# A recurrence and a feed-forward network on one core: the keys turned by one block transposition and a trip through DRAM

## The chip, the cores and the metric

The kernel runs on one core of a Trainium2 chip. The metric is device microseconds of one execution; lower is better. TensorE multiplies matrices, VectorE and ScalarE work element by element on 128 partitions, SyncE (SP) issues most transfers.

## The reference

For 4 batches of 8 heads, with 768 steps in time and 48 numbers a head, a state of 48 x 48 is decayed by rows and updated at each step, and read with the query. The outputs of all heads together are the rows of x, 3072 x 384, for a feed-forward network with 2048 hidden units.

```
for t in range(S):
    state = alpha[:, :, t, :, None] * state + einsum('bhd,bhe->bhde', k[:, :, t], v[:, :, t])
    y[:, :, t] = einsum('bhd,bhde->bhe', q[:, :, t], state)
x = y.transpose(0, 2, 1, 3).reshape(B * S, H * D)
h = x @ w_in
out = (0.5 * h * (1.0 + erf(h / sqrt(2)))) @ w_out
```

All inputs and the output are float32.

## The kernel before

**The attention.** The work is cut into 24 units: 12 groups of 256 steps (three for each batch), each in two units of four heads. A unit holds two tiles of 128 partitions, 64 for each head (48 in use). VectorE makes running products of alpha forward and backward (L314, L327), multiplies queries (L320) and keys (L333) with them, and the recurrence becomes products of matrices over chunks of 64 steps. In `scores` (L354) keys meet queries; VectorE masks the result (`masked`, L400). In `inside`, the masked scores meet the values (L423), and the keys meet the values (L441), which gives what each chunk adds to the state. For L441 the keys must lie with time on the partitions; this turned form is the tile kn. VectorE adds the states up (`chain`, L461), and in `outside_part` (L491) the states meet the queries. ScalarE copies the outputs out (`y_out`, L571), to free the bank of PSUM for the next scores; they become rows of x in two parts, a rounded one and a rest (L563, L567).

**How the keys are turned.** Units 0 to 5 use TensorE (L362) and a copy by ScalarE. Units 6 to 23 (FLIPPED = 6) use VectorE: `flipped` (L373) transposes 32 x 32 blocks, four of them in one instruction, from one group of 32 partitions to another. 16 instructions turn one unit; the plan places them in pairs ("flip").

**The feed-forward network.** Weights and activations are split into a rounded part and a rest, and three products are added. Rows 0 to 1023 go in blocks of 256 rows (L599, L691), the rest in wide blocks of 512 (L616, L634). A step is a first product, two passes of the activation on ScalarE (L668, L672), the rest of the activation on VectorE (L681, glo), and a second product. A wide block has 16 steps of 18 matmuls of 512 columns.

**The order of work.** All of it is written out ahead: a planner in the kernel gives each operation a cost (the table COST, in us), the operations that it waits for, and a rank, and simulates the engines. The order that comes out is the order in which the instructions are issued on TensorE, VectorE, ScalarE and SP. From unit 6 on TensorE visits the attention for the old state of unit n-2, `inside` of unit n-1 and the scores of unit n close together, and works on the network between these visits. When a unit's rows of x may be written depends on the network: the wide blocks have two buffers. Loads of later units and the transfers that spread rows of x over partitions (x<-z, L589) are issued by SP in the plan's order.

Of the kernel before, what the change touches and what calls it, by code (L numbers as in the profile page):

```python
# [8 lines left out]
F32 = mybir.dt.float32  # L9
# [16 lines left out]
FLIPPED = 6  # L26
# [9 lines left out]
SLOW = 1.0  # L36
COST = dict(
    turn=0.3, head=0.75, body=0.95, tail=0.49, sel=0.6, sel2=1.0, ends=0.22, differ=1.2, half=0.34, minus=0.4, gminus=0.35, rest=0.5, rest2=1.0,
    scan=0.65, scan2=0.65, back0=0.86, back=0.71, times=0.62, q=1.35, scores=1.24, scores1=0.69, flip=0.54, kn=0.52, mask=0.62, mask1=0.4, kn1=0.36, inside=1.28, chain=1.1, outer=0.77, carry=0.22,
    xh=0.6, xl=0.72, spread=2.0, check=0.85, load=2.6, fetch=0.4, u=1.0, c0=0.56, c1=0.89, c2=0.56, c3=0.95, c4=0.92,  # L40
    hi=0.82, lo=0.89, gemm1=2.12, gelu=0.51, low=0.62, most=1.4, last=0.69, part=1.0,
    wide1=2.1, wide2=2.07, wpart=1.1,
# [5 lines left out]
def gla_then_gelu_ffn(ctx: ExitStack, tc: tile.TileContext, q, k, v, alpha, qg, kg, ag, vg, w_in, w_out, out):  # L48
    nc = tc.nc
    B, H, D, S = q.shape  # L50
    NF, P, NK, _ = w_in.shape
# [5 lines left out]
    NCH = G // CS  # L57
    DP = 64
    NPAIR = H // 2
    NU = NPAIR // 2  # L60
    DR = DP - D
    QUAD = P // 4
# [9 lines left out]
    const = ctx.enter_context(tc.tile_pool(name="const", bufs=1))  # L72
    work = ctx.enter_context(tc.tile_pool(name="work", bufs=3))
    ffn = ctx.enter_context(tc.tile_pool(name="ffn", bufs=2))
    ps_s = ctx.enter_context(tc.tile_pool(name="ps_s", bufs=1, space=PSUM))
    y_cm = tc.tile_pool(name="ps_y", bufs=1, space=PSUM, side="right")
    ps_y = y_cm.__enter__()
# [43 lines left out]
    def y_of(n):  # L121
        return (ybank, sbank)[n % 2] if n < SPLIT else sbank
# [10 lines left out]
    cur = {}  # L133
# [31 lines left out]
    mask = const.tile([P, CS], F32, name="mask")  # L165
    nc.gpsimd.memset(mask, 1.0)
    for half in range(2):
        r = slice(half * CS, (half + 1) * CS)
        nc.gpsimd.affine_select(  # L169
            out=mask[r],  # L170
            in_=mask[r],
# [47 lines left out]
    for f2 in range(NF2):  # L219
        src = w_in[2 * f2 : 2 * f2 + 2].rearrange("two p c f -> p two (c f)")  # L220
        pieces.append((src, wi_hi[f2], wi_lo[f2]))
        src = w_out[2 * f2 * P : (2 * f2 + 2) * P, :].rearrange("(two p) e -> p two e", p=P)
# [114 lines left out]
    def ends_batch(g, j):  # L337
        return g % GPB == GPB - 1 and j == NCH - 1

    def scores(g, u):  # L340
        d = cur[g, u]
        n = NU * g + u
        d["s"] = s_of(n)
        if n >= SPLIT:
            d["s"] = [
                ps_h().tile([P, BANK], F32, tag="hp", name=f"sh_{n}"),
                ps_w().tile([P, BANK], F32, tag="sw", name=f"sw_{n}"),
            ]
        for j in range(NCH):
            for i in range(2):  # L350
                t, o = slice(j * CS, (j + 1) * CS), slice(i * CS, (i + 1) * CS)
                for h in range(2):
                    r = slice(h * DP, h * DP + D)
                    nc.tensor.matmul(  # L354
                        d["s"][h][o, t], lhsT=d["kt"][r, (2 * j + i) * CS : (2 * j + i + 1) * CS], rhs=d["qt"][r, i, t], start=True, stop=True
                    )

    def turned(g, u):
        d = cur[g, u]
        for j in range(NCH):  # L360
            e = (2 + j % 2) * C
            nc.tensor.transpose(  # L362
                out=d["s"][j // 2][:, e : e + C], in_=d["kt"][:, 2 * j * CS : 2 * (j + 1) * CS], identity=ident
            )

    def flipped(g, u, src, dsts):

        k5 = cur[g, u]["kt"].rearrange("p (j i a t) -> p i a j t", j=NCH, i=2, a=2)
        n5 = kn_tile(g, u).rearrange("p h (j b d) -> p h b j d", j=NCH, b=2)
        r = slice(src * QUAD, (src + 1) * QUAD)  # L370
        for dst in dsts:
            o = slice(dst * QUAD, (dst + 1) * QUAD)
            nc.vector.transpose(out=n5[o, src // 2, src % 2], in_=k5[r, dst // 2, dst % 2])  # L373

    def room(n):
        return stage if n % 2 and n < NU * NSB else work

    def kn_tile(g, u):
        d = cur[g, u]
        if "kn" not in d:  # L380
            pool = room(NU * g + u)
            d["kn"] = pool.tile([P, 2, 2 * P], F32, tag="kn", bufs=2 if pool is work else 1, name=f"kn_{g}_{u}")
        return d["kn"]
# [23 lines left out]
    def inside(g, u):  # L407
        d = cur[g, u]
        ybank = y_of(NU * g + u)
        vn = vbuf[g % NB]  # L410
        spare = () if g else (0, 1)[: u + 1]
        for i in spare:
            nc.tensor.matmul(
                ybank[:, i, :G], lhsT=zeros, rhs=products[:, :G], start=True, stop=False, skip_group_check=True
            )
        for j in range(NCH):
            for i in range(2):
                r = slice(i * CS, (i + 1) * CS)
                for h in range(2):
                    rows = D if i in spare else DP  # L420
                    o = slice((h ^ i) * DP, (h ^ i) * DP + rows)
                    e = (2 * u + h) * D
                    nc.tensor.matmul(  # L423
                        ybank[o, i, j * CS : (j + 1) * CS],
                        lhsT=vn[r, j, e : e + rows],
                        rhs=d["ss"][r, h, j, :],
                        start=(j == 0 and i not in spare),
                        stop=(j == 0 and g % GPB == 0),
                        skip_group_check=True,
                    )  # L430
        kn = d["kn"].rearrange("p b (c h d) -> p b c h d", c=2, h=2)
        for j in range(NCH):
            if ends_batch(g, j):
                continue
            t = 2 * C + j * D
            for i in range(2):
                r = slice(i * CS, (i + 1) * CS)
                for h in range(2):
                    o = slice(h * DP, (h + 1) * DP)
                    e = (2 * u + h) * D  # L440
                    nc.tensor.matmul(  # L441
                        ybank[o, i, t : t + D],
                        lhsT=d["kn"][r, h, j * DP : (j + 1) * DP] if NU * g + u >= FLIPPED else kn[r, j // 2, j % 2, h],
                        rhs=vn[r, j, e : e + D],
                        start=False,
                        stop=True,
                        skip_group_check=True,
                    )
# [400 lines left out]
    def op(*args, **kw):  # L849
        ops.append(Op(*args, **kw))  # L850
        return ops[-1]
# [4 lines left out]
    def plan_unit(n):  # L856
        g, u = divmod(n, NU)
        d = unit[n] = {}
        p, pp_ = unit.get(n - 1, {}), unit.get(n - 2, {})
        r = unit_rank[n]  # L860
# [23 lines left out]
        shared = [pp_.get("out", pp_["xh"]), pp_.get("out", pp_["xl"])] if NU <= n <= SPLIT else []  # L884
        of_y = [yp.get("out", yp.get(x)) for x in ("xh", "xl")]
        if n >= FLIPPED:
            for src in range(4):
                for dsts in ((0, 1), (2, 3)):
                    d["kn"] = op("DVE", "flip", lambda src=src, dsts=dsts: flipped(g, u, src, dsts), [d["keys"], pp_["inside"]], rank=r)
            d["scores"] = op("PE", "scores1", lambda: scores(g, u), [d["keys"], d["q"], sp.get("mask"), sp.get("kn") if n < FLIPPED + NU else None, *shared], rank=r)  # L890
        else:
            d["scores"] = op("PE", "scores", lambda: (scores(g, u), turned(g, u)), [d["keys"], d["q"], sp.get("mask"), sp.get("kn"), *shared], rank=r)
# [27 lines left out]
        else:  # L920
            d["mask"] = op("DVE", "mask", lambda: masked(g, u), [d["scores"], rp.get("inside")], rank=-1)
            d["kn"] = op("ACT", "kn", lambda: turned_out(g, u), [d["scores"], rp.get("inside"), d["mask"]], rank=-1)
        d["inside"] = op("PE", "inside", lambda: inside(g, u), [d["mask"], *of_y], rank=r)
        if n >= NU:
            d["inside"].deps.append(d["kn"])
# [77 lines left out]
    for n in range(n_units):  # L1003
        plan_unit(n)
# [224 lines left out]
    t = 0.0  # L1229
    idle = 0  # L1230
    while True:
        moved = False
        for e in ("DVE", "ACT", "PE", "SP", "POOL"):
            if free_at[e] <= t + 1e-9:
                o = choose(e, t)
# [13 lines left out]
        t = min(later_on)  # L1249
# [8 lines left out]
    for o in plan:  # L1258
# [5 lines left out]
        out=outside[:, n_units:],  # L1264
# [90 lines left out]
```

## Time and profile before

| | |
|---|---|
| three runs | 497.4, 499.94, 499.95 us; median 499.94 us |
| the profiled execution | 500.8 us, of which the span of the profile is 499.1 us |
| granted clock of TensorE over the span | 0.995 |
| TensorE, matmuls | busy 482.2 us, 5144 instructions |
| VectorE | busy 336.3 us, 773 instructions |
| ScalarE | busy 192.2 us, 381 instructions |
| transfers | 44.31 MB, mean 89 GB/s |

Busy times are unions of the time in which an engine has an instruction under way. Matmuls are pipelined and their ends are modelled, so a new one starts long before the one before it ends. In the rows, PE is TensorE, PEld its weight loads, DVE VectorE, ACT ScalarE; L373 is line 373 of the kernel.

### The profile page before, as it was taken

To read this page: it belongs to the slowest core of one execution; us is meant where nothing else is said; L and a number is where in the kernel's file an instruction comes from. 1 tells how busy PE (TensorE), PEld (TensorE's weight loads), DVE (VectorE), ACT (ScalarE), POOL (GpSimd) and SP (SyncE) were. 2 spreads that over 40 slices of the span, in tenths; PEclk is the share of its full clock that TensorE was granted. 3 is DMA by queue.
4 is the path that set the end of the run, shared out by engine and by line. 5 is a ranking of instruction groups with operands and counts; after the bars stand their busy time and mean duration, and the time that the engine had idled before them with its cause. 6 is when DMAs were issued, how large, how long until landed. Compare 5 with 4: busy or idle time off the path is not lost.

```text
span 499.1 us, 12166 instructions
## 1 busy us (share of the span) xinstructions
PE 482.2 (97%) x5144; PEld 409.2 (82%) x5144; DVE 336.3 (67%) x773; ACT 192.2 (39%) x381; POOL 7.4 (1%) x21
## 2 busy tenths in 40 slices
PE   7999999999999999999999999999999999999993
PEld 5678999999989999777788777778778888888882
DVE  6898998989999999999943999941751111211112
ACT  4788765243343334332423343232432222322221
POOL 2000000000000000000000000000000000000000
PEclk9999999999999999999999999999999999999997
DMA  8996662322232232313200622000100000100001
GB/s 299 393 348 198 247 211 71 108 78 85 85 93 97 92 110 71 130 54 107 73 1 1 198 69 88 4 1 1 70 24 5 1 1 0 65 0 0 1 0 69
DMA packets 20845, 44.31 MB, mean 89 GB/s; under 512 B 2832, under 2 KB 4688, under 8 KB 20784
## 3 DMA queue, kind: packets, MB, share of 16 engines
q1 hardware_dynamic: 19136, 38.41, 22.9%
q0 software_dynamic: 880, 3.93, 2.0%
q10 hardware_dynamic: 768, 1.11, 0.7%
q8 instruction: 42, 0.69, 0.5%
q14 instruction: 19, 0.16, 0.1%
HBM read 36.57 MB, written 4.72 MB: 83 GB/s over the span
## 4 chain that ended last, share of the span: by engine, by line
PE 51%; DVE 29%; DMA 7%; issue 6%; ACT 4%; ACTq 1%; SPq 0%; DVEq 0%
PE hw L616 22%; PE accw L634 22%; DVE kn L373 10%; DMA st<-in_moe_w_out_dram 5%; DVE glo L681 4%; DVE pp L314 3%; DVE rp L327 2%; PE hp L599 2%; DVE state L461 2%; PE acc L691 1%; DVE kd L333 1%; DMA x<-z 1%; DVE ss L400 1%; DMA ad<-in_ag_dram 1%; DVE x L567 1%
## 5 line engine op out<-in xcount | busy, mean ns | idle before, releaser
L681 DVE TENSOR_TENSOR glo<-hw,ghi 128x512 fp32r<-128x512 f32 x64 | 44.1, 689 | 133.2 <-ACT hw L672 132.8
L616 PE MATMUL hw<-x,wih 128*128 128x512 f32 x384 | 121.2, 396 | 0.6 <-DVE ss L400 0.6
L668 ACT ACTIVATE ghi<-hw 128x512 fp32r<-128x512 f32 x64 | 38.3, 599 | 176.6 <-PE hw L616 176.6
L373 DVE STREAM_TRANSPOSE kn<-kd 32x128 f32<-32x128 f32 x288 | 87.1, 303 | 4.4
L616 PEld LDWEIGHTS hw<-x,wih 128*128 128x128 f32 x384 | 71.4, 188 | 17.9 <-PE hw L616 1.0
L634 PE MATMUL accw<-ghi,woh 128*128 128x512 f32 x192 | 76.3, 398 | 0.0
L616 PE MATMUL hw<-x,wil 128*128 128x512 f32 x192 | 75.8, 395 | 0.0
L634 PE MATMUL accw<-ghi,wol 128*128 128x512 f32 x192 | 75.2, 392 | 0.0
L599 PE MATMUL hp<-x,wih 128*128 128x256 f32 x384 | 69.7, 282 | 0.0
L599 PEld LDWEIGHTS hp<-x,wih 128*128 128x128 f32 x384 | 59.9, 188 | 0.5 <-issue 0.2
L634 PE MATMUL accw<-glo,woh 128*128 128x512 f32 x192 | 56.7, 397 | 0.8 <-DVE glo L681 0.8
L599 PE MATMUL hp<-x,wil 128*128 128x256 f32 x192 | 53.6, 280 | 0.0
L691 PE MATMUL acc<-woh,ghi 128*128 128x384 f32 x128 | 44.0, 344 | 0.8 <-ACT ghi L668 0.8
L616 PEld LDWEIGHTS hw<-x,wil 128*128 128x128 f32 x192 | 36.0, 187 | 8.8
L691 PE MATMUL acc<-wol,ghi 128*128 128x384 f32 x128 | 43.1, 337 | 0.0
L634 PEld LDWEIGHTS accw<-ghi,woh 128*128 128x128 f32 x192 | 36.0, 187 | 8.5
L634 PEld LDWEIGHTS accw<-glo,woh 128*128 128x128 f32 x192 | 35.4, 188 | 8.8 <-DVE glo L681 1.2
L634 PEld LDWEIGHTS accw<-ghi,wol 128*128 128x128 f32 x192 | 36.1, 188 | 7.7
L668 ACT ACTIVATE ghi<-hp 128x512 fp32r<-128x512 f32 x32 | 19.1, 596 | 55.4 <-PE hp L599 46.0
L672 ACT ACTIVATE hw<-hw 128x512 f32<-128x512 f32 x64 | 37.9, 593 | 0.0
L599 PEld LDWEIGHTS hp<-x,wil 128*128 128x128 f32 x192 | 36.1, 188 | 0.0
L314 DVE TENSOR_TENSOR_SCAN pp<-ad,bottom 128x256 f32<-128x256 f32 x48 | 31.5, 680 | 4.6 <-POOL mask L169 3.5
(136 smaller groups left out, 584.6 us busy)
## 6 DMA issues: line engine op xcount, KB each, us to landing
st<-in_moe_w_in_dram SPq DMA_DIRECT2D x8, 768.0 KB, 7.4
st<-in_moe_w_out_dram SPq DMA_DIRECT2D x8, 768.0 KB, 7.7
qd<-in_qg_dram SPq DMA_DIRECT2D x23, 256.0 KB, 3.1
ad<-in_ag_dram SPq DMA_DIRECT2D x23, 256.0 KB, 3.0
kd<-in_kg_dram SPq DMA_DIRECT2D x23, 256.0 KB, 3.5
vn<-in_vg_dram SPq DMA_DIRECT2D x12, 416.0 KB, 4.7
out_dram<-parts POOLq DMA_DIRECT2D x3, 768.0 KB, 3.8
x<-z SPq DMA_DIRECT2D x60, 32.0 KB, 2.0
```

The source lines that it names most:

```text
L314: nc.vector.tensor_tensor_scan(pp[:, i], at[:, i], bottom, MID, ALU.mult, ALU.max)
L327: nc.vector.tensor_tensor_scan(rp[:, i, G - 2 :: -1], at[:, i, G - 1 : 0 : -1], bottom[:, 1:], rp[:, i, G - 1 :], ALU.mult, ALU.max)
L333: nc.vector.tensor_tensor(out=k4, in0=k4, in1=cur[g, u]["rp"].rearrange("p i (j t) -> p i j t", j=NCH), op=ALU.mult)
L373: nc.vector.transpose(out=n5[o, src // 2, src % 2], in_=k5[r, dst // 2, dst % 2])
L461: d["chain"] = nc.vector.tensor_tensor(out=st[j + 1], in0=new, in1=st[j], op=ALU.add)
L599: nc.tensor.matmul(hp[:, j, :], lhsT=a[:, j, i * P : (i + 1) * P], rhs=x[:, i, :], start=(start and m == 0), stop=(stop and (j, i, n) in t ...
L616: nc.tensor.matmul(h, lhsT=a[:, j, i * P : (i + 1) * P], rhs=x[:, i, part], start=(i == 0 and n == 0), stop=(i == NK - 1 and n == 2),)
L634: nc.tensor.matmul(acc[i], lhsT=w[:, j, e], rhs=a, start=(f == 0 and k == 0 and w is wo_hi[f2]), stop=(f == NF - 1 and k == 1),)
L668: nc.scalar.activation(ghi, hp, AF.Gelu)
L672: nc.scalar.activation(hp, hp, AF.Gelu)
L681: nc.vector.tensor_tensor(out=glo, in0=hp, in1=ghi.bitcast(F32), op=ALU.subtract)
L691: nc.tensor.matmul(acc[t], lhsT=a[:, j, t * C : (t + 1) * C], rhs=w[:, j, :], start=(first and j == 0 and k == 0 and w is wo_hi[f]), stop= ...
```

## The change

From unit 6 on, one VectorE instruction transposes all 32 x 32 blocks of a unit in place, that is, without moving a block to other partitions, and writes them to the tile fl. One transfer writes fl to a tile in DRAM, and four read it back, one for each group of 32 partitions, so that the blocks land where they belong. The tile kn that they fill has the index of the chunk innermost: `kn[time, half, d, chunk]`. The weights of the state products at L441 are `kn[r, h, :, j]`. The planner gets costs for the three new operations in place of the old one; "move" and "moves" are SP's.

```diff
--- before.py
+++ after.py
@@ -36,7 +36,7 @@
 SLOW = 1.0
 COST = dict(
     turn=0.3, head=0.75, body=0.95, tail=0.49, sel=0.6, sel2=1.0, ends=0.22, differ=1.2, half=0.34, minus=0.4, gminus=0.35, rest=0.5, rest2=1.0,
-    scan=0.65, scan2=0.65, back0=0.86, back=0.71, times=0.62, q=1.35, scores=1.24, scores1=0.69, flip=0.54, kn=0.52, mask=0.62, mask1=0.4, kn1=0.36, inside=1.28, chain=1.1, outer=0.77, carry=0.22,
+    scan=0.65, scan2=0.65, back0=0.86, back=0.71, times=0.62, q=1.35, scores=1.24, scores1=0.69, flip=0.66, move=0.35, moves=1.4, kn=0.52, mask=0.62, mask1=0.4, kn1=0.36, inside=1.28, chain=1.1, outer=0.77, carry=0.22,
     xh=0.6, xl=0.72, spread=2.0, check=0.85, load=2.6, fetch=0.4, u=1.0, c0=0.56, c1=0.89, c2=0.56, c3=0.95, c4=0.92,
     hi=0.82, lo=0.89, gemm1=2.12, gelu=0.51, low=0.62, most=1.4, last=0.69, part=1.0,
     wide1=2.1, wide2=2.07, wpart=1.1,
@@ -72,6 +72,7 @@
     const = ctx.enter_context(tc.tile_pool(name="const", bufs=1))
     work = ctx.enter_context(tc.tile_pool(name="work", bufs=3))
     ffn = ctx.enter_context(tc.tile_pool(name="ffn", bufs=2))
+    bounce = ctx.enter_context(tc.tile_pool(name="bounce", bufs=2, space=bass.MemoryType.DRAM))
     ps_s = ctx.enter_context(tc.tile_pool(name="ps_s", bufs=1, space=PSUM))
     y_cm = tc.tile_pool(name="ps_y", bufs=1, space=PSUM, side="right")
     ps_y = y_cm.__enter__()
@@ -363,14 +364,27 @@
                 out=d["s"][j // 2][:, e : e + C], in_=d["kt"][:, 2 * j * CS : 2 * (j + 1) * CS], identity=ident
             )
 
-    def flipped(g, u, src, dsts):
-
-        k5 = cur[g, u]["kt"].rearrange("p (j i a t) -> p i a j t", j=NCH, i=2, a=2)
-        n5 = kn_tile(g, u).rearrange("p h (j b d) -> p h b j d", j=NCH, b=2)
-        r = slice(src * QUAD, (src + 1) * QUAD)
-        for dst in dsts:
-            o = slice(dst * QUAD, (dst + 1) * QUAD)
-            nc.vector.transpose(out=n5[o, src // 2, src % 2], in_=k5[r, dst // 2, dst % 2])
+    def flipped(g, u):
+
+        d = cur[g, u]
+        d["fl"] = work.tile([P, 4, QUAD, NCH], F32, tag="fl", bufs=1, name=f"fl_{g}_{u}")
+        nc.vector.transpose(
+            out=d["fl"].rearrange("p q d j -> p q j d"), in_=d["kt"].rearrange("p (j i a t) -> p (i a) j t", j=NCH, i=2, a=2)
+        )
+
+    def flip_out(g, u):
+        d = cur[g, u]
+        d["fd"] = bounce.tile([P, 4, NCH * QUAD], F32, tag="fd", name=f"fd_{g}_{u}")
+        nc.sync.dma_start(d["fd"], d["fl"].rearrange("p q d j -> p q (d j)"))
+
+    def flip_back(g, u):
+        d = cur[g, u]
+        d["kn"] = work.tile([P, 2, DP, NCH], F32, tag="kn", bufs=2, name=f"kn_{g}_{u}")
+        for dst in range(4):
+            nc.sync.dma_start(
+                d["kn"][dst * QUAD : (dst + 1) * QUAD].rearrange("t h (b d) j -> t (h b) (d j)", b=2),
+                d["fd"].rearrange("(s t) q e -> q t s e", t=QUAD)[dst],
+            )
 
     def room(n):
         return stage if n % 2 and n < NU * NSB else work
@@ -428,7 +442,8 @@
                         stop=(j == 0 and g % GPB == 0),
                         skip_group_check=True,
                     )
-        kn = d["kn"].rearrange("p b (c h d) -> p b c h d", c=2, h=2)
+        if NU * g + u < FLIPPED:
+            kn = d["kn"].rearrange("p b (c h d) -> p b c h d", c=2, h=2)
         for j in range(NCH):
             if ends_batch(g, j):
                 continue
@@ -440,7 +455,7 @@
                     e = (2 * u + h) * D
                     nc.tensor.matmul(
                         ybank[o, i, t : t + D],
-                        lhsT=d["kn"][r, h, j * DP : (j + 1) * DP] if NU * g + u >= FLIPPED else kn[r, j // 2, j % 2, h],
+                        lhsT=d["kn"][r, h, :, j] if NU * g + u >= FLIPPED else kn[r, j // 2, j % 2, h],
                         rhs=vn[r, j, e : e + D],
                         start=False,
                         stop=True,
@@ -884,9 +899,9 @@
         shared = [pp_.get("out", pp_["xh"]), pp_.get("out", pp_["xl"])] if NU <= n <= SPLIT else []
         of_y = [yp.get("out", yp.get(x)) for x in ("xh", "xl")]
         if n >= FLIPPED:
-            for src in range(4):
-                for dsts in ((0, 1), (2, 3)):
-                    d["kn"] = op("DVE", "flip", lambda src=src, dsts=dsts: flipped(g, u, src, dsts), [d["keys"], pp_["inside"]], rank=r)
+            flip = op("DVE", "flip", lambda: flipped(g, u), [d["keys"], p.get("away")], rank=r)
+            d["away"] = op("SP", "move", lambda: flip_out(g, u), [flip], rank=r - 50, lands=2.2, kb=262)
+            d["kn"] = op("SP", "moves", lambda: flip_back(g, u), [d["away"], pp_["inside"]], rank=r - 50, lands=2.2, kb=262)
             d["scores"] = op("PE", "scores1", lambda: scores(g, u), [d["keys"], d["q"], sp.get("mask"), sp.get("kn") if n < FLIPPED + NU else None, *shared], rank=r)
         else:
             d["scores"] = op("PE", "scores", lambda: (scores(g, u), turned(g, u)), [d["keys"], d["q"], sp.get("mask"), sp.get("kn"), *shared], rank=r)
```

## Rows read from the trace of the kernel before

**Rows 1.** Busy us (count) by stretch: PE, PEld, DVE, ACT, POOL; clock, DMA, GB/s

```profile
74.00:166.00 92.00, 89.70 (x1376) 86.26 (x1375) 86.93 (x217) 36.28 (x77) 2.33 (x3) 1.00 0.29 92
166.00:370.00 204.00, 202.13 (x2285) 165.50 (x2286) 160.58 (x408) 68.44 (x143) 1.84 (x3) 1.00 0.20 63
370.00:490.00 120.00, 120.00 (x537) 97.06 (x528) 22.10 (x33) 32.69 (x60) 0.53 (x1) 1.00 0.03 9
```

**Rows 2.** Waits of TensorE, 74 to 490 us: total, times, longest

```profile
PE acc L691 <- DVE glo L681: 1.3, 3, 0.6
PE ybank L354 <- ACT yc L571: 0.9, 1, 0.9
PE accw L634 <- DVE glo L681: 0.8, 1, 0.8
PE hw L616 <- DVE ss L400: 0.6, 1, 0.6
PE sbank L354 <- ACT yc L571: 0.6, 1, 0.6
```

**Rows 3.** Timeline of TensorE at one stop: start, us

```profile
147.93 0.52 PE L441 MATMUL ybank<-vn,kn 64*64 64x48 f32 x24
149.00 0.69 PE L354 MATMUL sbank<-qd,kd 48*64 48x64 f32 x32 [0.55 <-ACT yc L571]
```

**Rows 4.** Busy time of VectorE by stretch, line L373 alone

```profile
74.00:166.00 92.00, 31.46 (x104) 1.00 0.29 92
```

**Rows 5.** Timeline of TensorE: beginning of two neighbouring visits

```profile
121.85 0.55 PE L491 MATMUL sbank<-qd,state 48*48 48x64 f32 x24
...
136.06 0.67 PE L491 MATMUL ybank<-qd,state 48*48 48x64 f32 x32
```

**Rows 6.** Busy times by stretch, as rows 1

```profile
260.00:280.00 20.00, 20.00 (x146) 16.11 (x145) 9.74 (x20) 7.85 (x15) 0.35 (x1) 1.00 0.12 35
```

**Rows 7.** Groups of VectorE's instructions: busy us, mean ns

```profile
L373 DVE STREAM_TRANSPOSE kn<-kd 32x128 f32<-32x128 f32 x288 | 87.1, 303 | 4.4
...
L333 DVE TENSOR_TENSOR kd<-kd,rp 128x512 f32<-128x512 f32 x24 | 16.6, 690 | 0.6
...
L285 DVE TENSOR_TENSOR wil<-st,wih 128x768 fp32r<-128x768 f32 x7 | 6.7, 951 | 0.2 <-ACT wih L282 0.2
```

**Rows 8.** Groups of TensorE's weight loads

```profile
L599 PEld LDWEIGHTS hp<-x,wih 128*128 128x128 f32 x384 | 59.9, 188 | 0.5 <-issue 0.2
...
L441 PEld LDWEIGHTS sbank<-vn,kn 64*64 64x64 f32 x528 | 9.5, 135 | 0.0
```

**Rows 9.** Timeline of weight loads in one visit

```profile
147.41 0.56 PEld L423 LDWEIGHTS ybank<-ss,vn 64*64 64x64 f32 x32
147.88 0.45 PEld L441 LDWEIGHTS ybank<-vn,kn 64*64 64x64 f32 x24
```

**Rows 10.** Busy time of matmuls and weight loads by stretch, line L441 alone

```profile
74.00:166.00 92.00, 4.08 (x200) 3.59 (x200) 1.00 0.29 92
166.00:370.00 204.00, 7.13 (x352) 6.29 (x352) 1.00 0.20 63
```

**Rows 11.** The chain that ended last, 250 to 262 us

```profile
254.19 4.13 PE accw L634 x18
```

**Rows 12.** Groups of ScalarE's instructions

```profile
L668 ACT ACTIVATE ghi<-hw 128x512 fp32r<-128x512 f32 x64 | 38.3, 599 | 176.6 <-PE hw L616 176.6
...
L268 ACT CAST top<-st 128x768 f16<-128x768 bf16 x16 | 17.3, 1080 | 9.3 <-DMA st<-in_moe_w_out_dram 5.4 <-DMA st<-in_moe_w_in_dram 3.8
```

**Rows 13.** Transfers: size of one, median us to landing

```profile
qd<-in_qg_dram SPq DMA_DIRECT2D x23, 256.0 KB, 3.1
...
x<-z SPq DMA_DIRECT2D x60, 32.0 KB, 2.0
...
out_dram<-parts SPq DMA_DIRECT2D x2, 256.0 KB, 3.6
```

**Rows 14.** Timeline of SP: four issues

```profile
182.23 2.50 SPq L589 DMA_DIRECT2D x<-z  x4
```

## The prediction

> **What bounds the kernel now.** I read the busy times by stretch first [rows 1]. From 74 us, where the first unit with turned keys begins, to 490 us TensorE is busy for 411.8 of 416 us at a granted clock of 1.00; VectorE is at 87 of 92 us until 166 us and falls to 22 of 120 us at the end. Both look full in the middle, so the next question is who waits for whom. TensorE's waits from 74 to 490 us come to 4.2 us in seven stops, all behind VectorE or behind a ScalarE copy [rows 2]. A stop is a little longer than its row: the last of the 24 state products that begin at 147.93 starts, at their spacing of 14.7 ns, near 148.27, the next matmul at 149.00; the row says 0.55 us idle where some 0.7 us were lost [rows 3], because the modelled end of a matmul covers some 0.16 us. Seven such remainders make it 5.3 us. So TensorE's work sets the end, and VectorE sets only how fast the units of the linear attention advance beside it.
>
> That second statement can be checked. In 74 to 166 us VectorE's transpositions take 31.5 of its 86.9 us, 104 of them, thus 6.5 units' worth [rows 1, 4]. Everything else is 55.5 us, 8.5 us a unit; with 4.8 us of transpositions a unit costs 13.4 us. Two neighbouring visits of TensorE to the attention stand 14.2 us apart [rows 5]. The units are VectorE's, the end is TensorE's. Later even VectorE is not full: in 260 to 280 us it is busy 9.7 of 20 us [rows 6], because a unit may not write its rows of x before the feed-forward steps of an older block have read theirs, and these steps are TensorE's.
>
> **What the change removes.** 16 transpositions of 32x128 at 303 ns [rows 7] go, 18 times: 87.1 us of VectorE. In their place stands one of 128x512. A 128x512 product takes 690 ns and a 128x768 one 951 ns [rows 7], 1.02 ns an element a partition; that is also the most that the 128 elements of the old transposition can take, since it leaves 173 ns for the start. So the new one takes about 0.17 + 512 x 1.04 = 0.70 us. It writes words 16 bytes apart, which no row shows on VectorE; at four times the rate it would be 2.3 us. VectorE gets back 2.5 to 4.1 us a unit, 46 to 74 us in all. On the path this is worth only TensorE's stops. Of the 5.3 us I leave out the one of 0.9 + 0.16 us behind ScalarE's copy at 78.6 us, where the first new unit has hardly begun, and take back 4.2 us. The bounds are 0 and 5.3 us: a new order of the plan can make as many stops as it removes.
>
> The unit's time on VectorE falls to 8.5 + 0.7 = 9.2 us, somewhat less as fewer feed-forward steps share it. The attention runs ahead until it has to wait for x. The blocks of the feed-forward part are not fewer for that, so nothing at the end gets shorter.
>
> **What it adds on TensorE.** The weights of the state products at L441 are now read with a step of four words, as the chunk index has become the innermost one. These weight loads are on the critical engine. What a column costs is seen in two rows: 128 columns take 188 ns, 64 take 135 [rows 8], 0.83 ns each. The loads of the four quadrants overlap: 32 of L423 pass in 0.47 us [rows 9], 58.7 ns for four, of which 64 x 0.83 = 53 ns is the streaming of the columns. So the loads, and not the 48 columns that move, pace L441. There are 552 such matmuls after 74 us, 24 of them the last old unit's [rows 10]: 528, in groups of four 132.
>
> The price of the step is not in the trace, and is bounded so. Nothing: VectorE's 951 ns stands for an operand read at a step of two words, and the slope is the same as without. Four times: three of four neighbouring words are read in vain, 132 x 3 x 53 ns = 21 us. The nearest row of TensorE itself is the fastest reading that it shows: 18 matmuls of 512 words in 4.13 us [rows 11], 229 ns for 512 words, 1.79 ns for each fresh stretch of four words. A weight column at the new step needs a fresh stretch each; at that rate it costs 1.79 in place of 0.83 ns, 61 ns more a group, 132 x 61 ns = **8.1 us**. I take this value, because no row shows TensorE fetching such stretches faster, and ScalarE too is slower with steps: 768 halves of words, read and written one by one, take it 1080 ns, 1.41 ns each, against 599 ns for 512 words in line, 1.17 ns each with the start counted in [rows 12].
>
> The VectorE row would say that a step is free. [...]
>
> **What it adds on the queues.** SP gets five transfers a unit, 90 in all: one of 256 KB out, then four of 64 KB back, which wait for the landing of the first. Of the rows, 256 KB to DRAM land in 3.6 us, 256 KB from DRAM in 3.1, small transfers in 2.0 [rows 13]. SP spends 2.5 us on issuing four [rows 14]. From the end of the keys: 0.7 + 0.1 for the transposition, 3.1 to 3.6 out, 0.1, then three issues of 0.63 before the last one, and 2.0 to 3.1 for it: 8.0 to 9.5 us. The state product needs them one visit later, and the next unit's keys are about 9 us behind. So the path through DRAM is just covered by the attention's own pace, and where x is waited for, by far more. While SP waits for the outgoing transfer, the loads of later units and the copies of x rows stand behind it for some 3 us; the loads have waited in the old order too, and the copies of x serve blocks that TensorE has not come to. I charge 0.5 us; the bounds are 0 and 15 us, ten visits late by 1.5 us.
>
> **The sum**, against the profiled execution's 500.8 us: 500.8 - 4.2 + 8.1 + 0.5 = 505.2 us. The profiled execution is 0.9 us over the median of 499.94, so I write 504.3 us: 0.9% slower. Changes below 0.5% (2.5 us) I take as not told from none.
>
> **Rivals.** *The weight step is free.* For it: the VectorE row, and loads that start well ahead of their matmuls. Against it: 53 of 58.7 ns are streaming, so any slower column shows. Then 500.8 - 4.2 + 0.5 - 0.9 = 496.2 us, faster; this decides once a column costs less than 1.1 ns instead of 1.79. *The weight step costs all four words.* For it only the bound: 505.2 + 13 - 0.9 = 517 us. *The transfers are late.* The state product waits for the last landing, and the scores and feed-forward steps that the plan puts behind it on TensorE wait with it. It begins once the path is over about 9 us; at 1.5 us over on ten visits 504.3 + 14.5 = 519 us with the step, 511 without. Against it: rows of landings that agree within a microsecond. *VectorE's time does not shrink* (2.3 us for the new transposition): it changes nothing by itself, as 2.5 us a unit still come back.
>
> **How the numbers follow.** The priced step: 0.50, with 500 to 508 us for itself, the ends being stops that are all new (+4.2) and a charge of half (-4). Free step: 0.35. Four words: 0.07. Late transfers: 0.08. The range of 495.0 to 509.5 us holds the first two almost whole and a part of the last. Faster: three quarters of the free step and a trace of the first, 0.27. Same, 497.4 to 502.4 us: a fifth of the free step and a third of the first, 0.23. Slower: the rest, 0.50.
>
> **What would show it.** The new profile should have 18 transpositions of 128x512 near 0.7 us and VectorE busy some 75 us less; the attention's visits 9 us apart from unit 6 on, and earlier waits for x. The weight loads of L441 should take some 61 ns more than 135, and 32 of them about 0.95 us in place of 0.47. TensorE's waits behind the difference at L681 and the copy at L571 should nearly go. It is wrong if these loads keep their 135 ns, if TensorE waits for the landing of kn, or if the saved VectorE time shortens the end, which would mean that TensorE's busy time hid more waiting than the spacing of its matmuls shows.

## The result and the profile after

The changed kernel takes 502.26 us (median of five runs, 502.08 to 502.58), the one before 499.94 us (five runs, 497.4 to 500.44). The ratio is 1.0055 with a 95% interval of 1.0032 to 1.0078: 2.8 us slower, give or take 1.2; the two medians differ by 2.3 us. The profiled execution took 502.26 us with a span of 500.7 us, 1.6 us more than the span before.

The page of the changed kernel gives busy time, share of the span and number of instructions for each engine:

```profile
PE 487.6 (97%) x5144; PEld 417.6 (83%) x5144; DVE 267.4 (53%) x503; ACT 191.8 (38%) x381; POOL 7.4 (1%) x21
```

VectorE is busy 68.9 us less and the end is later. TensorE and its weight loads have gained busy time, at the same number of matmuls. The stretches, with the columns of [rows 1]; the last line answers to [rows 6]:

```profile
74.00:166.00 92.00, 91.25 (x1634) 88.02 (x1633) 83.85 (x165) 39.62 (x89) 1.61 (x2) 1.00 0.56 171
166.00:370.00 204.00, 203.74 (x1984) 170.10 (x1985) 92.63 (x183) 63.74 (x130) 2.57 (x4) 1.00 0.24 74
370.00:490.00 120.00, 120.00 (x549) 96.85 (x548) 23.13 (x38) 32.52 (x61) 0.53 (x1) 1.00 0.03 9
260.00:280.00 20.00, 20.00 (x147) 16.10 (x146) 9.12 (x16) 7.85 (x15) 0.04 (x1) 1.00 0.09 25
```

From 166 to 370 us VectorE now works 92.6 of 204 us, before 160.6. In the first stretch it stays full, but it passes more units there: 264 state products against 200 [rows 10]. These are the transposition and the weight loads of the state products among the groups and one line's own summary (ns, least, median and most; it covers the old units too), and one visit in the timeline of the weight loads, against [rows 7 to 9]. L437 is the product of scores and values (L423 before), L456 the state products (L441 before):

```profile
L371 DVE STREAM_TRANSPOSE fl<-kd 128x512 f32<-128x512 f32 x18 | 19.9, 1107 | 0.5
...
L456 PEld LDWEIGHTS sbank<-vn,kn x528: 133/213/213, 16.6 to 369.4; 64*64 64x64 f32 x176
```

```profile
107.52 0.56 PEld L437 LDWEIGHTS ybank<-ss,vn 64*64 64x64 f32 x32
107.98 1.09 PEld L456 LDWEIGHTS ybank<-vn,kn 64*64 64x64 f32 x32
```

A weight load takes 213 ns (the median) where it took 135, and 32 of them 1.09 us where the 32 of L437 beside them, whose words lie in line, take 0.56. The rate shows when the last load is left out: before, 24 loads in 0.45 us [rows 9] are (0.45 - 0.135) / 23 = 13.7 ns each, 55 ns for a group of four quadrants; now (1.09 - 0.213) / 31 = 28.3 ns, 113 ns a group, 1.77 ns a column.

TensorE's waits from 74 to 490 us, against [rows 2] (us in total, times, longest):

```profile
PE ybank L355 <- ACT yc L586: 0.8, 1, 0.8
PE acc L706 <- DVE glo L696: 0.3, 1, 0.3
```

Two are left of seven, and none is for kn. The visits to the attention, in TensorE's timeline, against [rows 5]:

```profile
98.28 0.55 PE L506 MATMUL ybank<-qd,state 48*48 48x64 f32 x24
...
107.20 0.55 PE L506 MATMUL sbank<-qd,state 48*48 48x64 f32 x24
```

8.9 us lie between these two; the next follow at 116.2, 126.6 and 135.5 us. From unit 6 until 195 us the visits stand 7.4 to 11.5 us apart; then none comes until 278 us, where before they went on until 245 us and resumed at 277. The transfers (size of one, median us to landing), against [rows 13], and SP's issues in one visit, against [rows 14]:

```profile
kd<-in_kg_dram SPq DMA_DIRECT2D x23, 256.0 KB, 5.3
...
fd<-fl SPq DMA_DIRECT2D x18, 256.0 KB, 2.1
kn<-fd SPq DMA_DIRECT2D x72, 64.0 KB, 4.2
x<-z SPq DMA_DIRECT2D x60, 32.0 KB, 2.9
```

```profile
116.32 0.34 SPq L378 DMA_DIRECT2D fd<-fl  x1
...
118.33 3.25 SPq L384 DMA_DIRECT2D kn<-fd  x4
```

Loads and copies land later than before: kd in 5.3 us instead of 3.5, the copies of x in 2.9 instead of 2.0. The trip is the cause: in the run below that does without it they land in 3.6 and 2.0 us.

Adding up the times from one matmul's start to the next, by line, says where the 1.6 us of span lie: the state products +5.4 us, the wide blocks' two products -2.5, the scores' products with values -0.4, the stretch behind the start of the last matmul -0.9. Of the rest no line moved by more than 0.3 us, and together these cancel. The +5.4 is the price of the step less the stops that stood at these products before: from one state product to the next in the same visit the starts lie 26.5 ns apart on average, before 13.3 ns, which is 7.0 us over all of them.

### The profile page after: what moved, and what is told of

Read it like the earlier page. It is cut to its first block, busy times and chain, and to the rows that moved or that the text cites. A ratio compares the mean times of both kernels' runs of the same rounds, so it can differ in the third digit from the quotient of the medians.

```text
span 500.7 us, 12052 instructions
## 1 busy us (share of the span) xinstructions
PE 487.6 (97%) x5144; PEld 417.6 (83%) x5144; DVE 267.4 (53%) x503; ACT 191.8 (38%) x381; POOL 7.4 (1%) x21
## 4 chain that ended last, share of the span: by engine, by line
PE 85%; DMA 6%; DVE 3%; ACT 3%; issue 1%; ACTq 0%; SPq 0%
PE hw L631 27%; PE accw L649 27%; PE acc L706 11%; PE hp L614 10%; DMA st<-in_moe_w_out_dram 4%; PE sbank L456 3%; PE sbank L437 2%; PE sbank L506 2%; DMA qd<-in_qg_dram 1%; PE sh L355 1%; ACT top L269 1%; PE ybank L456 1%; DVE glo L696 1%; DVE st L273 1%; DVE rp L328 0%
## 5 line engine op out<-in xcount | busy, mean ns | idle before, releaser
L696 DVE TENSOR_TENSOR glo<-hw,ghi 128x512 fp32r<-128x512 f32 x64 | 44.2, 690 | 185.0 <-ACT hw L687 185.0
L328 DVE TENSOR_TENSOR_SCAN rp<-ad,rp,bottom 128x255 f32<-128x255 f32 x48 | 34.0, 739 | 0.9
```

The lines of the kernel that those rows point to most:

```text
L328: nc.vector.tensor_tensor_scan(rp[:, i, G - 2 :: -1], at[:, i, G - 1 : 0 : -1], bottom[:, 1:], rp[:, i, G - 1 :], ALU.mult, ALU.max)
L696: nc.vector.tensor_tensor(out=glo, in0=hp, in1=ghi.bitcast(F32), op=ALU.subtract)
```

## The experiments

Theory: two sums of opposite sign. The step of four words costs TensorE some 7 or 8 us, VectorE's relief gives some 4 us of stops back, and the trip through DRAM costs nothing. The rivals are these: the time is lost by the trip (its transfers late, or its queue full), or the relief is worth nothing and other small changes of the order add up to the difference.

**Everything in line.** The tile kn is laid out by chunk, so that weights are read and blocks written in line, that is, without a step. The transposition's blocks then go out in pieces of 128 bytes, by four transfers in place of one; four bring them back. The planner's costs for SP stay those of the change.

```diff
+        d["fl"] = work.tile([P, 4, NCH // 1, QUAD, 1], F32, ...)
+        for s in range(4):
+            nc.sync.dma_start(
+                d["fd"].rearrange("t q c s x -> s t (q c) x")[s],
+                d["fl"][s * QUAD : (s + 1) * QUAD].rearrange("t q c d e -> t (q c) (d e)"),
+            )
...
-                        lhsT=d["kn"][r, h, :, j] if ...
+                        lhsT=d["kn"][r, j // 1, h, :, j % 1] if ...
```

> The changed kernel with the chunk index no longer innermost: the new transposition writes in line and the weights at the state products are read in line. The trip through DRAM stays, in eight transfers a unit in place of five and in pieces of 128 bytes on the way out. Theory A (a weight column at a step of four words costs a fresh stretch of 16 bytes, 1.8 ns in place of 0.83): 32 weight loads of the state products take 0.47 us again, and the time is 502.3 - 8.1 = 494.2 us, below the kernel before. Theory B (the loss is in the trip through DRAM or the new order of the plan): 502 us or more. Both expect the transposition at 0.70 us if VectorE pays for the step too.

It took 510.8 us, ratio 1.022 (1.0178 to 1.0263). The groups of the transposition and of the weight loads, and among TensorE's waits the one for kn:

```profile
L371 DVE STREAM_TRANSPOSE fl<-kd 128x512 f32<-128x512 f32 x18 | 12.8, 710 | 0.5
L460 PEld LDWEIGHTS sbank<-vn,kn 64*64 64x64 f32 x528 | 10.8, 139 | 3.8 <-DMA kn<-fd 3.2 <-issue 0.4
```

```profile
PE sbank L460 <- DMA kn<-fd: 2.8, 2, 2.2
```

Both steps' prices are gone: the transposition takes 710 ns in place of 1107, and a weight load 139 ns on average, where the change's median is 213. But new stops took back more than that: TensorE's waits from 74 to 490 us sum to 9.5 us, in the change to 1.1. Only the 2.8 us shown are for kn; the others are for activations, masked scores and ScalarE's copies, in an order that was planned for faster issues. Behind the longest stop the granted clock was at half for 6.8 us (0.50 from 120 to 126 us; see the last section). Theory A's 494.2 us were missed and theory B's 502 us or more came, but by stops that the change does not have. So the time says nothing about the step, and the next runs separate the two.

**Halves in line.** The same five transfers as in the change, with blocks that stay 32 columns wide and are written in line: each state product is cut into two of 32 columns, whose weights lie in line.

```diff
+                        for b in range(2):
+                            nc.tensor.matmul(
+                                ybank[h * DP + b * QUAD : h * DP + (b + 1) * QUAD, i, t : t + D],
+                                lhsT=d["kn"][r, h, b, j],
...
```

> The changed kernel with blocks of 32 words in line, the same five transfers in pieces of 512 bytes, and each state product cut into two of 32 output rows, since the 64 columns then lie in two runs. Theory A: weights in line; twice the instructions at 6.7 ns each, eight in 54 ns, still fit under the 58.5 ns of a group: 494.2 us. If a half costs as much as a whole, 132 x 58.5 ns = 7.7 us come back: 502 us. Theory B: 502 us or more.

500.21 us (12 runs), ratio 1.001 (0.9999 to 1.0022). The group of the half loads:

```profile
L458 PEld LDWEIGHTS sbank<-vn,kn 64*32 64x32 f32 x880 | 9.5, 105 | 1.1
```

Twice the loads, each of half the columns and 105 ns, cost less than the step: 2 us under the change. Both forecasts were missed, 494.2 us for halves that cost half and 502 us for halves that cost a whole: the starts of two halves lie 9.9 ns apart on average, 19.7 ns for a whole product, between the 13.3 ns in line and the 26.5 ns at the step. TensorE's only wait is one of 0.2 us. The transposition writes in line here (710 ns), so two things differ from the change; the runs with columns in line, below, change the weights alone.

**The step alone.** The kernel before, its 16 transpositions and its order of work, with kn laid out with the chunk innermost. No trip, no relief.

```diff
-        n5 = kn_tile(g, u).rearrange("p h (j b d) -> p h b j d", j=NCH, b=2)
+        n5 = kn_tile(g, u).rearrange("p h (b d j) -> p h b j d", j=NCH, b=2)
-                        lhsT=d["kn"][r, h, j * DP : (j + 1) * DP] if ...
+                        lhsT=d["kn"][r, h].rearrange("p (d j) -> p d j", j=NCH)[:, :, j] if ...
```

> The kernel before with one thing of the change: the 16 transpositions write with the chunk index innermost, and the weights of the state products are read at the step of four words. No trip through DRAM, the same order. Theory A: the state products cost 8.1 us more; the transpositions, which now write at the step, take about 0.1 us more each, 1.6 us a unit, which VectorE passes on as some more stops: 508 to 511 us. Theory B: 500 us, or a little more through VectorE alone.

527.36 us, ratio 1.0563 (1.0539 to 1.0586), far over the forecast of 508 to 511 us and more than the weights can cost: the state products' starts lie 26.2 ns apart, 6.9 us over before. The transposition's group, and TensorE's two largest waits:

```profile
L373 DVE STREAM_TRANSPOSE kn<-kd 32x128 f32<-32x128 f32 x288 | 115.2, 400 | 4.4
```

```profile
PE acc L691 <- DVE glo L681: 8.3, 8, 2.1
PE accw L634 <- DVE glo L681: 6.8, 5, 2.5
```

VectorE's writes pay for the step as well, 400 ns in place of 303, 28 us in all. TensorE's waits from 74 to 490 us sum to 17.1 us, before to 4.2 [rows 2], and in two stretches of 3.4 us the granted clock was at half (a mean of 0.59 from 238 to 242 us and of 0.66 from 346 to 351 us; see the last section). One edit loaded two engines, and the plan knew of neither; a later run tells it of VectorE's.

**Two chunks interleaved.** Between the two layouts: pairs of chunks side by side, so that a column of weights is two words from the next, and outgoing pieces of 256 bytes, again eight transfers.

```diff
+        d["fl"] = work.tile([P, 4, NCH // 2, QUAD, 2], F32, ...)
...
+                        lhsT=d["kn"][r, j // 2, h, :, j % 2] if ...
```

> As the run in line, but two chunks interleaved: weights are read, and blocks written, at a step of two words. [...] If the price grows evenly with the step (a third of it at two words): 494.2 + 2.7 = 497 us.

508.48 us, ratio 1.0171 (1.0147 to 1.0195). The weight loads take 135 ns and the transposition 711, as in line. The forecast of 497 us was missed, and the time is lost as in the run in line: TensorE's waits sum to 10.3 us. SP's timeline shows the issues for one unit, TensorE's its wait for these blocks:

```profile
108.20 2.55 SPq L380 DMA_DIRECT2D fd<-fl  x4
...
113.69 1.72 SPq L389 DMA_DIRECT2D kn<-fd  x4
```

```profile
117.13 0.65 PE L442 MATMUL sbank<-ss,vn 64*64 64x64 f32 x32
119.61 0.88 PE L461 MATMUL sbank<-vn,kn 64*64 64x48 f32 x30 [1.83 <-DMA kn<-fd]
```

Four issues of the outgoing blocks take 2.5 us, and the planner had been told 0.35; four loads of a later unit are issued before the way back begins. From 108.2 to 123.1 us issue follows issue with hardly a gap.

**Columns in line, blocks as they are.** The change with one expression altered: the weights are read in line from the same tile, and are thus other columns than the right ones. Order, transposition, step of its writes and trip stay.

```diff
-                        lhsT=d["kn"][r, h, :, j] if ...
+                        lhsT=d["kn"][r, h].rearrange("p d j -> p (d j)")[:, j * DP : (j + 1) * DP] if ...
```

> The changed kernel with one thing undone: the state products read 64 words in line from the same tile, which are other columns than the right ones, so the output's numbers are not the reference's. Transposition, trip through DRAM and order stay. Theory A (the loss is the weight step): 502.3 - 8.1 = 494.2 us. Theory B (the trip or the plan's order costs as much as VectorE's relief brings): 502 us.

**No trip.** The transposition writes its blocks straight to kn, with the step of four words; blocks are not exchanged, and SP gets no transfers.

```diff
         nc.vector.transpose(
+            out=d["kn"].rearrange("p h (b d) j -> p (h b) j d", b=2), in_=...
...
-            d["away"] = op("SP", "move", ...)
-            d["kn"] = op("SP", "moves", ...)
+            d["kn"] = op("DVE", "flip", lambda: flipped(g, u), [d["keys"], pp_["inside"]], rank=r)
```

> The changed kernel without the five transfers: the blocks are not exchanged between partitions, the state products read them where VectorE put them, at the step of four words; the output's numbers are not the reference's. If the trip is covered by the attention's pace: 502 us as with it. If it costs as the late-transfer rival says: below 500 us. The step alone would then leave it 3 to 4 us over the kernel before.

**Neither trip nor step in the weights.** Both edits together.

> Neither the trip nor the weight step (blocks not exchanged, other columns read in line; the output's numbers are not the reference's): what VectorE's relief alone is worth. Theory A: 494 us, the same as with the trip and in line, since only the 4.7 us of TensorE's stops can come back. If VectorE's relief could shorten more than the stops: well below 494 us.

| ratio to before (95% interval), us | weights at a step of four | weights in line |
|---|---|---|
| with the trip | 1.0055 (1.0032 to 1.0078), the change, 502.26 | 0.9924 (0.9904 to 0.9943), 495.25 |
| without | 1.008 (1.0065 to 1.0094), 503.12 | 0.9935 (0.9918 to 0.9952), 495.94 |

Each ratio is to the runs of the kernel before that were taken beside it. Down the columns the trip costs nothing; by the ratios it is even 0.1 to 0.25% on the good side, and the intervals overlap. Along the lines the step in the weights costs 1.31% and 1.45%, 6.5 and 7.2 us. What is left without it, 0.9924 and 0.9935, is what VectorE's relief brings with the order that was planned for it: 3.2 to 3.8 us. The two were not taken apart. The two groups in which the step could show, in the run with columns in line:

```profile
L371 DVE STREAM_TRANSPOSE fl<-kd 128x512 f32<-128x512 f32 x18 | 19.9, 1107 | 0.5
L456 PEld LDWEIGHTS sbank<-vn,kn 64*64 64x64 f32 x528 | 9.6, 135 | 0.0
```

The transposition keeps its 1107 ns there, and only the weight loads differ from the change. So the 0.4 us a unit more on VectorE are not what the step costs.

**Step of two words, the planner told.** The run with two chunks interleaved, and three numbers of the plan set nearer to what its own trace showed of SP: 2.5 us for the four issues out, 1.7 us and more for the four back, 4.1 us to their landing.

```diff
-    ... move=0.35, moves=1.4, ...
+    ... move=2.5, moves=1.9, ...
-            d["kn"] = op("SP", "moves", ..., lands=2.2, kb=262)
+            d["kn"] = op("SP", "moves", ..., lands=3.5, kb=262)
```

> The run at a step of two words again, with its eight transfers told to the planner: 2.5 us of SP for the way out, 1.9 us back, landing 3.5 us after. If its 508.5 us came from a plan that believed in 0.35 us for four issues: TensorE's waits for kn go, and the weights at the step of two words cost as in line: 495 to 498 us. If the queue itself is full: 505 us or more.

495.79 us, ratio 0.994 (0.9922 to 0.9957): faster than both kernels, from 508.48 by the order of work alone. The groups, a visit's weight loads in the timeline, and all of TensorE's waits from 74 to 490 us:

```profile
L371 DVE STREAM_TRANSPOSE fl<-kd 128x512 f32<-128x512 f32 x18 | 12.8, 712 | 0.6
L461 PEld LDWEIGHTS sbank<-vn,kn 64*64 64x64 f32 x528 | 9.8, 135 | 0.0
...
109.78 0.59 PEld L461 LDWEIGHTS ybank<-vn,kn 64*64 64x64 f32 x32
```

```profile
PE ybank L355 <- ACT yc L591: 1.0, 2, 0.7
PE sbank L442 <- ACT yc L591: 0.3, 1, 0.3
```

The 32 loads are back at 0.59 us from 1.09, and no wait is for kn. The step of two words leaves a small trace, 13.9 ns between the starts of state products in place of 13.3, some 0.3 us in all.

**The outgoing blocks issued by GpSimd.** The same, with the four transfers out on another queue.

```diff
-            nc.sync.dma_start(
+            nc.gpsimd.dma_start(
-            d["away"] = op("SP", "move", ..., lands=2.2, kb=262)
+            d["away"] = op("POOL", "move", ..., lands=3.0, kb=262)
```

> The version with a step of two words whose planner knows the real costs of SP's transfers (495.8 us), with the four outgoing transfers of a unit issued by GpSimd instead of SP. Theory (SP is full but its delay is hidden once the plan knows it): no change, 495 to 497 us, weight loads 135 ns, no wait of TensorE for kn. Rival (SP's 5 us of issues a unit still hold back the spreading of x and the loads): 1 to 2 us faster, 494 us. Second rival (an issue by GpSimd takes longer and the blocks come back late): waits of TensorE for kn return, 498 us or more.

494.27 us, ratio 0.9901 (0.9887 to 0.9914), the fastest version here, 1.5 us under the run before it as the first rival had forecast. The two intervals (that of the run before it is 0.9922 to 0.9957) just miss each other. The landings of the transfers:

```profile
fd<-fl POOLq DMA_DIRECT2D x72, 64.0 KB, 2.6
kn<-fd SPq DMA_DIRECT2D x72, 64.0 KB, 2.8
```

The blocks land in 2.8 us, in the run before it in 3.9. In the two profiled executions the 1.3 us of span lie mostly in the stretch behind the start of the last matmul (6.9 instead of 8.0 us); the waits fell from 1.3 to 0.5 us. That stretch is anything from 6.9 to 8.1 us in the profiles of this study, so it is not shown that SP's share is what cost the last microsecond.

**The step alone, the planner told.** The run of the step alone, with one number: 0.74 us for a pair of transpositions.

```diff
-    ... flip=0.54, ...
+    ... flip=0.74, ...
```

> The kernel before with the step of four words in weights and in the writes of the 16 transpositions, as in the run of the step alone (527.4 us), but the planner is told 0.74 us for a pair of transpositions in place of 0.54. That run had 27 us more than before, of which the weights explain 8.2. Theory (VectorE's 28 us more do not fit beside the network, whatever the plan knows): 520 us or more. Rival (the plan's order was made for a faster VectorE, and TensorE ran into waits that another order avoids): 508 to 512 us, which is before plus the weights' 8, TensorE's stops back near 6 us from 25.

507.53 us, ratio 1.0167 (1.015 to 1.0184). The theory falls and the rival holds, a little below its range: 20 us were lost because the plan did not know of the slower transpositions. The page's VectorE is still 28.6 us busier than before, and its transposition as slow as in the untold run; the three waits of TensorE from 74 to 490 us:

```profile
PE 488.8 (97%) x5144; PEld 416.7 (82%) x5144; DVE 364.9 (72%) x773; ACT 192.9 (38%) x381; POOL 7.4 (1%) x21
...
L373 DVE STREAM_TRANSPOSE kn<-kd 32x128 f32<-32x128 f32 x288 | 115.1, 400 | 4.7
```

```profile
PE hw L616 <- DMA x<-z: 2.0, 1, 2.0
PE accw L634 <- DVE glo L681: 1.1, 2, 0.9
PE hp L599 <- DVE ss L400: 0.3, 1, 0.3
```

These waits sum to 3.4 us, before to 4.2. What remains over before is 1.67% or 8.3 us, give or take 0.8. The step in the weights is most of it: by the starts of the state products, 26.2 ns apart, it is 6.9 us here too. That leaves some 1.4 us for 28 us more on VectorE, once the planner was told of them.

**In line, the planner told.** The first run with the three numbers of the plan that stand above. The change itself was not run with such numbers; its waits of 1.1 us leave little to gain by them.

> The run with everything in line (510.8 us: weights and blocks without a step, eight transfers, outgoing pieces of 128 bytes) with the planner told what SP's issues and landings really take (2.5 and 1.9 us of SP, 3.5 us to the landing). Theory (there the loss was the plan's ignorance of SP, and a step of two words costs the same as none): 495 to 497 us, as the version with a step of two words, weight loads 135 ns, transposition 0.71 us, no waits for kn over 1 us. Rival (the small pieces of 128 bytes make the transfers slow): 500 us or more with TensorE waiting for kn.

496.32 us, ratio 0.9948 (0.9919 to 0.9976), from 510.8. In line is as good as a step of two words (0.994), and pieces of 128 bytes are no obstacle. The transposition takes 711 ns as there, and the weight loads:

```profile
L460 PEld LDWEIGHTS sbank<-vn,kn 64*64 64x64 f32 x528 | 9.6, 135 | 0.0
```

## Why the prediction was right, and where its terms were off

**TensorE sets the end, VectorE the pace of the units.** Right. 69 us less of VectorE bring 3 to 4 us, and 28 us more, with an order made for them, no more than some 1.4. The visits stand 9.7 us apart on average between 98 and 195 us, forecast 9 to 9.2. The attention comes to a halt at 195 us in place of 245, and goes on at the same time as before, near 278.

**The step in the weights, 8.1 us.** This was the term that set the sign, and it was right in kind and a little too large: 1.77 ns a column in the timeline against the 1.79 taken from TensorE's fastest streaming, 113 ns a group against 115. In the time it is 6.5 and 7.2 us in the two comparisons that keep the order of work, and 7.0 us by the starts of the state products. That the two rates agree does not show that one cause lies behind them. That a column at the step costs a fresh stretch of four words was the author's estimate; no run shows what is fetched. The runs show the price alone: at four words it is there on both engines (a load of 213 ns in place of 135, a transposition of 1107 ns in place of 710), at two words (135 and 711 ns) nearly nothing is left of it. The rival *the weight step is free* leaned on the row with a step of two words [rows 7], which was no evidence about four, and on loads that start ahead of their matmuls; at the step the loads pace these products all the same, 26.5 ns apart in place of 13.3.

**The stops taken back, 4.2 us.** Near: 3.2 to 3.8 us in the runs without the step in the weights. Of the seven waits one of the two behind ScalarE's copy stayed, 0.8 us, as was assumed, and one of 0.3 us behind L696 (L681 before).

**The transposition, 0.70 us.** Off: 1.107 us. The start and the rate that were read from other instructions hold to 1% where the write is in line (0.710); the step in the write, for which 2.3 us was the bound, costs (1107 - 710) / 512 = 0.78 ns an element more. The 67 us of transpositions that VectorE gets back, 69 us by its busy time, are inside the 46 to 74 that were given. The time did not notice, as the rival *VectorE's time does not shrink* said of a worse case.

**The trip, 0.5 us.** It costs nothing, though its parts were not as read: out 2.1 us instead of 3.1 to 3.6, back 4.2 instead of 2.0 to 3.1, while the loads of later units run beside it. From the keys to the last block it is 1.1 + 2.1 + 0.2 for the transposition, the way out and the starts, three issues of 3.25 / 4 us, and 4.2 back, 10.0 us where 8.0 to 9.5 were given; in the trace it is 6.6 to 11.8 us, the median 9.8. No state product waited for kn, but there is luck in it: the way out was read too long by 1.0 to 1.5 us and the way back too short by 1.1 to 2.2, and at 136 us the last block landed only 0.25 us ahead of the visit that needs it. The rival *transfers late* was to begin at a path of about 9 us; 13 of the 18 paths were longer, but the products that need the blocks came later still. It did not come in this kernel, but it was a real one: eight transfers in place of five, not told to the planner, made it come, and cost 2.3 and 2.7%, 12 and 14 us, over the same layouts with the planner told. Waits for kn itself were 4.2 and 2.8 us of that.

**The sum.** With the measured terms, 7 - 3.5 = 3.5 us, within the measured 2.8 ± 1.2; the forecast was 505.2 - 500.8 = 4.4. The difference is the 1 us of the step and the 0.5 us of the trip, less what the stops gave short. The forecast of 504.3 us for the median was 2 us too high. By the prediction's own line of 0.5% between slower and same the result lies on the edge: the ratio 1.0055 is just over it, the 502.26 us just inside the band of 497.4 to 502.4 us. That it is slower at all is clear of the interval. The profiled execution of the kernel before was 0.9 us over its median, that of the kernel after lies on its median; the 1.6 us of span between them therefore say less than the ratio.

## What to carry to other kernels

Before a layout puts an index innermost, ask at what step each later reader and writer meets it: here a step of four words made each column of a weight load take twice as long, 1.77 ns in place of 0.83, on the engine that sets the end, and turned a gain of 0.7% into a loss of 0.5%. Pairs instead of fours, with three more transfers and a plan that knew them, kept the gain. Where an order is planned from a table of costs, put the durations of the trace into it before judging a variant: the same operations, planned with better numbers, ran 12 to 20 us faster. Try an edit's parts apart, and price first the one on the engine that sets the end; the engine that lost 69 us of work was not it.

## What the runs showed of the hardware that was not expected

VectorE's write paid for the step nearly as TensorE's read did: the 128x512 transposition took 710 ns in line and 1107 ns at four words. With the prediction's 173 ns for the start, an estimate, an element goes from some 1.05 to 1.82 ns, near the 1.77 ns a column of TensorE's loads. TensorE's load at a step of four words was not four times as slow but twice, from 0.83 [rows 8] to 1.77 ns a column.

In three runs a stop of TensorE was followed by half the clock: in the two with eight transfers that the planner wasn't told of, and in that of the step alone. With two chunks interleaved TensorE stood idle for 1.83 us until 119.6 us; the windows behind it, with the columns of [rows 1], and its timeline then:

```profile
117.00:121.00 4.00, 2.17 (x118) 2.00 (x108) 1.91 (x6) 1.85 (x6) 0.00 (x0) 0.94 0.40 86
121.00:124.00 3.00, 3.00 (x21) 2.88 (x15) 2.52 (x7) 0.39 (x2) 0.00 (x0) 0.51 0.42 81
124.00:166.00 42.00, 38.99 (x689) 36.66 (x688) 32.04 (x67) 14.80 (x34) 0.74 (x1) 1.00 0.56 166
```

```profile
122.08 0.52 PE L711 MATMUL acc<-woh,ghi 128*128 128x384 f32 x1
122.40 0.52 PE L711 MATMUL acc<-wol,ghi 128*128 128x384 f32 x1
```

The granted clock is 0.51 until about 124 us, and matmuls of 384 columns follow each other by 0.32 us, where they do by 0.175 at a clock of 1.00: some 1.3 us on top of the stop. The length of the stop alone didn't decide it. In the told run of the step alone a stop of 2.0 us at 195 us was followed by a clock of 1.00, and in the untold one the clock fell behind a stop of 1.3 us at 345 us and not behind one of 1.6 us at 322 us. What decides was not tried.
